# Factors of the second half of the rows: transposed x levelled on VectorE in place of transposes on TensorE

## The chip, the cores and the metric

The kernel runs on one core of a Trainium2 chip. The metric is the device time of one execution in microseconds, lower being better. The kernel before took 1429.79 us, the median of three runs (1428.46 to 1429.94). The kernel writes the output of the reference with a few extra steps on the host side that only permute and copy inputs.

## What is computed

x has 2048 rows of 576 numbers (float32). It is normalised row by row, and two branches are added to it:

```python
xn = _layernorm(x, axis=-1)                     # (x - mean) / sqrt(var + 1e-5)
A  = irfft2(rfft2(xn) * (w_r + 1j * w_i))       # over rows and columns
B  = (sigmoid(xn @ w_gate) * (xn @ w_up)) @ w_down
return x + A + B                                # w_gate, w_up: 576 x 4608; w_down: 4608 x 576
```

Nearly all the arithmetic is in branch B. Matrices are multiplied in float32 accuracy by splitting each operand into a rounded high part and a low part and adding three products (high·high, low·high, high·low).

## The kernel before

**Products.** The 4608 hidden columns are cut into 36 blocks of 128 (`NF`), the rows into two halves of 1024 (`PAIRS`); a half has two chunks of 512 rows (`CW`). A *unit* `u` is one hidden block for one half: units 0 to 35 are the first half, 36 to 71 the second. In a unit both w_gate and w_up times both chunks are formed with seven products in place of eight (a scheme of Strassen's kind): `PRODS` names the seven pairs of factors. The x side has the factors A11, A12, A21, A22 (chunk 1 or 2, column half 1 or 2) and the sums S1 = A21 + A22, S2 = S1 − A11, S3 = A11 − A21, S4 = A12 − S2. They lie transposed (columns on the partitions) as high and low parts in the fixed tile `X`; A21 and S3 share a slot, since A21 is read only by the first two blocks. The first two blocks of each half (units 0 and 1, 36 and 37) are done with plain products (`plain`, four products for each block and chunk); from the third on `unit` runs the seven (`made(0)` to `made(6)`). Each product is seven matmuls (line 635) into a PSUM bank: A and B have one buffer, E has two.

**Down-projection.** `down` multiplies the hidden activations of two blocks with w_down for 128 rows (line 742, 12 matmuls into a tile of the PSUM pair `pp`, which has two buffers); VectorE adds the result to the accumulator (line 746). The activations are made at the end of a unit: VectorE adds (line 719) and multiplies by the gate (720), ScalarE rounds the high part `hh` (725), VectorE subtracts for the low part `hl` (726). Plain products use lines 658, 662, 663 and 664 for this.

**Factors of the second half.** `second_pair` begins at unit 35 (`NF - 1`). It opens a new room of buffers (`room("x")`), loads eight tiles of 128 rows (line 347), and after three turns `blocks(1, c)` normalises them on ScalarE (`prep`, line 409), splits the remainder of 32 columns (lines 391 and 396) and calls `fill` for A11, A12, A21 and A22. `fill` transposes 256 rows of one factor on TensorE with the identity (lines 438 and 439, six transposes into a PSUM pair), and copies the result to `X`: ScalarE the high part (442, 443), VectorE the low part (444). From the second plain product of the second half on, `factors(1)` forms the sums on VectorE (lines 421 to 424) and fills S1 and S2; `late(1)` fills S3 and S4 when the plain products are done. That is 16 fills.

**Order of the work.** The order is written out by hand. Within a unit `beside(i)` runs after product `i`: it puts in down-projections (`spots`), then calls `turn`, which takes two steps of making the next weights (`make`), one of w_down (`wd`), then pending adds, then one step of each generator in `sides`. For the second half `make` is `get_w`, which loads split weights from scratch memory. On top of that, at build time each engine's instructions are put in a queue by a scheduler with estimated durations: it takes the earliest written instruction that it believes ready, so an instruction can run well before its written place. `keep_in_program_order` pins an instruction behind the one written just before it on its engine. All loads go through the one SyncE queue.

**Buffers.** During the first half the room holds `raw` (two buffers, raw weights of one block each) and `xa` (four buffers). From unit 4 to 32 the statistics of the second half's rows are made (`later_stats`), and at unit 32 mean and reciprocal deviation of all rows are written as rows to the scratch tensor `rowd`, which the Fourier branch reads as well. That branch's first stage opens its own room at unit 39 (`stage1`).

The x side of the products reads transposed x for the Fourier branch already from an input `xt`, laid out on the host.

Of the kernel before, what the change touches and what calls it, by code (L numbers as in the profile page):

```python
# [9 lines left out]
F32 = mybir.dt.float32  # L10
F32R = mybir.dt.float32r
I32 = mybir.dt.int32
AF = mybir.ActivationFunctionType
OP = mybir.AluOpType
PSUM = bass.MemoryType.PSUM

P = 128
S, D, F = 2048, 576, 4608
KD = D // 2 + 1
NQ = KD + 1  # L20
N1, N2 = 64, 32
NT = S // P
EPS = 1e-5
HD = D // 2
FR = HD + 1 - 2 * P
CW = 512
TPC = CW // P
PAIRS = S // (2 * CW)
TPP = 2 * TPC
KT = 2  # L30
REM = HD - KT * P
NF = F // P
# [5 lines left out]
KR = 3 * REM  # L38
# [88 lines left out]
def _layout(x, w_r, w_i, w_gate, w_up, w_down):  # L127

    ks = np.concatenate([np.arange(KT * P), np.tile(np.arange(KT * P, HD), 4)])
    w = np.stack([w_gate[COLS], w_up[COLS]]).reshape(2, 2, HD, NF, P)[:, :, ks]  # L130
    w = w[[1, 1, 0, 0], [0, 1, 1, 0]].reshape(4, KT + 1, P, NF, P).transpose(3, 2, 0, 1, 4)
    v = np.stack([w_r, w_i])[:, :, KOF].reshape(2, N1, N2 // 2, 2, KD).transpose(2, 1, 0, 3, 4)
    v = np.broadcast_to(v[:, None], (N2 // 2, 2, N1, 2, 2, KD))
    x = x.reshape(S, D)[ROWS][:, COLS]
    xt = x.reshape(NT, P, 2, HD)[..., ks].reshape(NT, P, 2, KT + 1, P).transpose(0, 4, 2, 3, 1)
    lay = {"x": x.reshape(NT, P, D), "xt": xt.reshape(NT, P, 2 * (KT + 1) * P), "ri": v.reshape(N2 // 2, P, 4 * KD),
           "w": w.reshape(NF, P, 4 * (KT + 1) * P), "wd": w_down[:, COLS].reshape(NF, P, D)}
    return {k: np.ascontiguousarray(a) for k, a in lay.items()}

# [5 lines left out]


@with_exitstack
def spectral_glu_kernel(ctx: ExitStack, tc: tile.TileContext, x, xt, ri, w_in, w_down, out):
    nc = tc.nc
    con = {k: nc.inline_tensor(v, name=f"c_{k}").ap() for k, v in _constants().items()}  # L150

    def f32(ap):
        return ap.bitcast(F32)
# [17 lines left out]
    X = fix.tile([P, NX, 5, CW], F32R, name="X")  # L171
    XA = {k: i for i, k in enumerate(("A11", "A12", "S3", "A22", "S1", "S2", "S4"))}
# [10 lines left out]
    rowd = tc.dram_tile([2, NT, P], F32, name="rowd")  # L183
# [27 lines left out]
    R = {}  # L211
    fp = ExitStack()

    def room(k):
        fp.close()
        R["pool"] = pool = fp.enter_context(tc.tile_pool(name=f"p{k}", bufs=1, side="right", reuse_waits="tile"))
        return pool
# [128 lines left out]
    def load_x(dst, t):  # L346
        nc.sync.dma_start(dst, x[t])
# [35 lines left out]
    XS, XR, RM = {}, {}, {}  # L383

    def new_xs(p, m):
        XS[m] = R["pool"].tile([P, 5, HD], F32, tag="xa", name=f"xa{p}_{m}", bufs=TPC)
# [28 lines left out]
    def prep(p, m, c):  # L415
        prep_hi(p, m, c)
        prep_lo(m, c)
# [12 lines left out]
    def fill(p, k, mm):  # L430

        i, j0 = XA[k], XP[k]
        cols = slice(2 * mm * P, (2 * mm + 2) * P)
        pt = pair(f"px{p}_{k}_{mm}")
        for j in range(2):
            m = 2 * mm + j
            for q in range(KT):
                nc.tensor.transpose(pt[:, 0, (2 * q + j) * P:(2 * q + j + 1) * P], XS[m][:, j0, q * P:(q + 1) * P], idf)
            nc.tensor.transpose(pt[:KR, 1, j * P:(j + 1) * P].bitcast(F32R), XR[m, j0], idr)
        v = pt[:, 0].rearrange("p (q s) -> p q s", q=KT)  # L440
        o = X[:, i, :, cols]
        nc.scalar.activation(o[:, :KT], v, AF.Copy)
        nc.scalar.activation(o[:KR, KT], pt[:KR, 1, :2 * P], AF.Copy)
        nc.vector.tensor_tensor(o[:, KT + 1:], v, f32(o[:, :KT]), op=OP.subtract)  # L444
# [476 lines left out]
    pend, adds, sides = [], [], []  # L921
# [18 lines left out]
    def blocks(p, c):  # L940
        for mm in range(2):
            for m in (2 * mm, 2 * mm + 1):
                prep(p, m, c)
            for k in (1, 2):
                fill(p, f"A{c + 1}{k}", mm)
            yield

    def second_chunk():

        yield from make_p(1)  # L950
        yield from blocks(0, 1)

    def second_pair():

        room("x")
        for m in range(TPC):
            new_xs(1, m)
        for c in range(2):
            for m in range(TPC):
                load_x(XS[m][:, 2 * c:2 * c + 2].rearrange("p a d -> p (a d)"), TPP + c * TPC + m)  # L960
        for _ in range(3):
            yield
        for c in range(2):
            yield from blocks(1, c)

    def factors(p):

        for mm in range(2):
            for m in (2 * mm, 2 * mm + 1):
                sums(p, m)  # L970
                yield
            for k in ("S1", "S2"):
                fill(p, k, mm)
                yield
            if mm == 0:
                sides.append(late(p))

    def late(p):

        while not done[p]:  # L980
            yield
        for mm in range(2):
            for k in ("S3", "S4"):
                fill(p, k, mm)
            yield

    done = [False, False]
# [30 lines left out]
    for p in range(PAIRS):  # L1018

        calls = [(0, 0), (1, 0), (0, 1), (1, 1)] if p == 0 else [(0, 0), (0, 1), (1, 0), (1, 1)]  # L1020
        for n, (f, c) in enumerate(calls):
            u = p * NF + f
            if p == 0 and n >= 2:
                wd = make_d(f)
            elif p and c == 0:
                wd = get_d(u)
            if p == 0 and n == 0:
                sides.append(second_chunk())
            if n == 2 - p:
                sides.append(factors(p))  # L1030
            if p == 0 and n == 3:
                make = make_w(G)
            elif p and n in (0, 2):
                make = get_w(u + 1)

            def beside(i):
                for _ in range((0, 0, 2, 2, 0)[i] if p and n < 2 else 0):
                    if pend:
                        adds.append(down(*pend.pop(0)))
                if i >= 0:  # L1040
                    turn(3 if p == 0 else 1)

            plain(u, c, beside)
            if p == 0 and n == 0:
                finish(*sides)
                sides.clear()
                load_raw(2)
            if p == 0 and n == 1:
                load_raw(3)
            finish(wd)  # L1050
            if n == 3:
                finish(make)
        done[p] = True
        late_input[0] = False
        pend = [(p, 0, m) for m in range(TPP)]

        for f in range(G, NF):
            u = p * NF + f

            spots = {i: 1 for i in (range(5) if f % G else range(4, 7))}  # L1060
            if u == NF + G:

                spots = {3: 2, 4: 2, 5: 2, 6: 2}
            elif u == LAST - 2:
                spots = {i: 1 for i in range(2, 7)}
                pend = [(p, f // G - 1, m) for m in range(TPP)]
                sides.append(gather())
            elif u == LAST - 1:
                spots = {i: 1 for i in range(3)}
            if u + 1 < LAST:  # L1070
                make = make_w(u + 1) if u + 1 < NF else get_w(u + 1)
            if u < NF and f % G == 0:
                wd = make_dt(f // G)
            if p == 0 and f and f % 4 == 0:
                sides.append(later_stats(TPP + f // 4 - 1))
            if u == NF - 1:
                sides.append(second_pair())

            def beside(i):
                nonlocal step, rounds  # L1080
                if (u, i) == (NF + G + 1, 5):
                    rounds = seven()
                for _ in range(spots.get(i, 0)):
                    if pend:
                        adds.append(down(*pend.pop(0)))
                for a in extra.get((u, i), ()):
                    a()
                if i < 0:
                    return
                if u > NF + G:  # L1090
                    next(rounds, None)
                turn(2 if u + 1 < NF else 1)
                if u > NF + G:
                    active.extend(b() for b in begin.pop(step, []))
                    step += 1
                    aside()

            unit(u, beside)
            finish(make)
            if f % G == G - 1:  # L1100
                finish(wd)
            if u == NF + G:
                lower("b")
            if u + 2 < NF:
                load_raw(u + 2)
            if p == 0 and f % G == G - 1:
                pend = [(p, f // G, m) for m in range(TPP)]
# [30 lines left out]
```

## Time and profile before

| what | value |
|---|---|
| median of three runs | 1429.79 us (1428.46 to 1429.94) |
| the profiled execution's own time | 1428.53 us |
| its span, first to last instruction | 1426.7 us |
| mean granted TensorE clock | 0.998 |
| unit 34 starts / unit 35 starts / first product of unit 38 | 615.65 / 631.55 / 696.51 us |
| transposes of the second half's factors, first and last start | 644.33 / 701.87 us |

The profile comes from one execution on the chip. Times are microseconds from the first instruction; PE is TensorE, PEld its weight loads, DVE VectorE, ACT ScalarE, SP SyncE's queue. Matmuls overlap, so two neighbours in the timeline start closer together than one lasts: rates are read from start to start. In a wait row, the engine and line on the left stood idle until the one on the right was done.

### The profile page before, as it was taken

Reading aid. Unit: us, or ns where it says so; the run is one execution under the profiler, and the core shown is the slowest. Engines: PE = TensorE matmul, PEld = TensorE weight load, DVE = VectorE, ACT = ScalarE, POOL = GpSimd, SP = SyncE. Lnnn points to the kernel's source line nnn. Section 1 sums busy time; section 2 is a strip of 40 time slices with the busy share of each in tenths; the row PEclk is TensorE's granted clock in tenths of the full one; section 3 lists DMA queues with packets and bytes.
Section 4 is the critical chain, followed back from the end, with each engine's and each line's share of the span. In section 5 each row is a group of like instructions: output and inputs, shape, how many; then the busy total and the mean of one; then the engine's idle time right before and its main releaser. Section 6 shows DMA issues by size and latency. Waiting matters only on the chain. (4 is left out here: it accounts for less than half of the span.)

```text
span 1426.7 us, 20983 instructions
## 1 busy us (share of the span) xinstructions
PE 1412.8 (99%) x7979; PEld 1243.9 (87%) x7979; DVE 1097.7 (77%) x1734; ACT 651.2 (46%) x1075; POOL 3.3 (0%) x5
## 2 busy tenths in 40 slices
PE   8999999999999999999999999999999999999998
PEld 5888888888888888888888888888888889998997
DVE  7988888888888888766366888877888877766784
ACT  6644444444444444454335544534555534444431
POOL 0000000000000000000000000000000000000000
PEclk9999999999999999999999999999999999999999
DMA  6488677777777775564667777778888787776642
GB/s 249 192 329 309 257 270 264 271 262 270 265 262 265 256 265 223 224 262 149 233 215 231 232 217 236 217 250 261 274 267 274 239 284 232 234 222 199 200 126 83
DMA packets 130676, 341.41 MB, mean 239 GB/s; under 512 B 12144, under 2 KB 51600, under 8 KB 125712
## 3 DMA queue, kind: packets, MB, share of 16 engines
q1 hardware_dynamic: 129648, 338.76, 70.4%
q8 instruction: 63, 1.03, 0.3%
q10 hardware_dynamic: 928, 1.31, 0.3%
q14 instruction: 37, 0.30, 0.1%
HBM read 203.89 MB, written 136.13 MB: 238 GB/s over the span
## 5 line engine op out<-in xcount | busy, mean ns | idle before, releaser
L635 PE MATMUL pB<-X,w 128*128 128x512 f32 x1484 | 380.6, 393 | 0.0
L635 PEld LDWEIGHTS pB<-X,w 128*128 128x128 f32 x1484 | 267.6, 188 | 49.4 <-ACT v L699 1.3
L635 PE MATMUL pE<-X,w 128*128 128x512 f32 x1064 | 272.3, 392 | 0.0
L635 PE MATMUL pA<-X,w 128*128 128x512 f32 x1008 | 260.1, 394 | 1.8 <-DVE X L444 1.2
L635 PEld LDWEIGHTS pE<-X,w 128*128 128x128 f32 x1064 | 193.1, 188 | 34.2
L635 PEld LDWEIGHTS pA<-X,w 128*128 128x128 f32 x1008 | 184.0, 189 | 35.4 <-DVE X L444 1.9
L742 PE MATMUL po<-wd,hh 128*128 128x288 f32 x1216 | 210.9, 295 | 0.0
L833 PEld LDWEIGHTS ps<-wf,hs 128*128 128x128 f32 x1260 | 189.0, 188 | 17.8 <-ACT qs L841 0.9
L833 PE MATMUL ps<-wf,hs 128*128 128x288 f32 x1260 | 202.1, 295 | 0.4 <-ACT qs L841 0.4
L742 PEld LDWEIGHTS po<-wd,hh 128*128 128x128 f32 x1216 | 184.4, 188 | 11.3
L746 DVE TENSOR_TENSOR acc<-acc,po 128x576 f32<-128x576 f32 x168 | 125.9, 750 | 76.7 <-PE po L742 75.5
L239 ACT ACTIVATE w<-raw 128x768 fp32r<-128x768 f32 (+1 forms) x106 | 100.9, 953 | 92.7 <-PE pE L635 36.5
L742 PE MATMUL po<-wd,hl 128*128 128x288 f32 x608 | 128.9, 293 | 0.0
L843 DVE TENSOR_TENSOR qs<-qs,ps 128x576 f32<-128x576 f32 x112 | 84.1, 751 | 28.3 <-PE ps L833 27.5
L742 PEld LDWEIGHTS po<-wd,hl 128*128 128x128 f32 x608 | 98.8, 189 | 0.0
L700 DVE TENSOR_TENSOR y<-v,pE 128x512 f32<-128x512 f32 x68 | 46.8, 688 | 52.3 <-ACT v L699 51.3
L843 DVE TENSOR_TENSOR acc<-acc,ps 128x576 f32<-128x576 f32 x90 | 67.6, 751 | 23.2 <-PE ps L833 22.6
L241 DVE TENSOR_TENSOR w<-raw,w 128x512 fp32r<-128x512 f32 (+1 forms) x106 | 81.9, 773 | 3.2 <-ACT w L239 2.9
L720 DVE TENSOR_TENSOR y<-y,g 128x1024 f32<-128x1024 f32 x67 | 81.9, 1223 | 3.2
L769 ACT ACTIVATE hs<-y 128x512 fp32r<-128x512 f32 x105 | 64.8, 629 | 37.8 <-DVE y L720 14.6
L703 ACT ACTIVATE g<-pB 128x512 f32<-128x512 f32 x68 | 40.6, 598 | 90.4 <-PE pB L635 90.2
L699 ACT ACTIVATE v<-pB 128x512 f32<-128x512 f32 x68 | 40.6, 598 | 71.2 <-PE pB L635 70.7
(162 smaller groups left out, 1636.2 us busy)
## 6 DMA issues: line engine op xcount, KB each, us to landing
w<-wsp SPq DMA_DIRECT2D x246, 320.0 KB, 3.5
wsp<-w SPq DMA_DIRECT2D x34, 2240.0 KB, 7.7
raw<-in_w SPq DMA_DIRECT2D x34, 768.0 KB, 9.7
wdsp<-wd SPq DMA_DIRECT2D x36, 576.0 KB, 4.7
wf<-tsp SPq DMA_DIRECT2D x60, 288.0 KB, 3.8
wf<-wdsp SPq DMA_DIRECT2D x45, 288.0 KB, 3.9
std<-in_wd SPq DMA_DIRECT2D x36, 288.0 KB, 5.5
ri<-in_ri SPq DMA_DIRECT2D x16, 578.0 KB, 5.2
```

The source lines that it names most:

```text
L239: placed(nc.scalar.activation(o[:, :, :3, :], src, AF.Copy))
L241: placed(nc.vector.tensor_tensor(o[:, :, 3:, :], src[:, :, :KT, :], f32(o[:, :, :KT, :]), op=OP.subtract))
L635: nc.tensor.matmul(bank, w[:, sw, :], X[:, x, sx, :], start=start and j == 0, stop=stop and j == len(STEPS) - 1, skip_group_check=skip)
L699: nc.scalar.activation(v[:, 1], bank["B"], AF.Copy)
L700: nc.vector.tensor_tensor(y[:, 1], v[:, 1], bank["E"], op=OP.add)
L703: nc.scalar.activation(g[:, 1], bank["B"], AF.Sigmoid)
L720: nc.vector.tensor_tensor(y, y, g, op=OP.mult)
L742: nc.tensor.matmul(pd[:, b, :HD], h[i], w[k][b], start=g == 0 and n == 0, stop=g == G - 1 and n == 2)
L746: nc.vector.tensor_tensor(a, a, pd[:, :, :HD], op=OP.add)
L769: nc.scalar.activation(hs[:, 0], src, AF.Copy)
L833: nc.tensor.matmul(pd[:, i, :HD], h[:, a, m], w[:, b], start=q == 0, stop=q == 2)
L843: nc.vector.tensor_tensor(o, o, pd[:, :, :HD], op=OP.add)
```

## The change

A second layout of transposed x for the second half of the rows, `xg`, is an input: for each chunk and column half the columns on the partitions and the chunk's 512 rows along the free dimension, two blocks of 128 columns and one with the remainder of 32 columns repeated four times. The raw numbers are loaded and normalised where they lie: mean and reciprocal deviation of the 512 rows are read from `rowd` onto all partitions (`load_rows`), and VectorE subtracts and multiplies (`level`). `put` writes high and low parts into `X`; `second_factors` forms the sums on the transposed data. No transposes remain for the second half, and `room("x")` is not opened: chunk 0 and the rows of both chunks lie in the `xa` buffers (`spare`), chunk 1 in the two `raw` buffers (`load_whole`). The first chunk is loaded at the start of unit 34 and levelled in its turns 2 to 5; the rows of chunk 1 and its second column half are loaded at the start of unit 35, where chunk 1 is levelled and A11, A12, A21, A22 are put, each after the product that last reads its slot. S1, S2 and S4 follow beside the plain products, S3 after them.

```diff
--- before.py
+++ after.py
@@ -133,7 +133,8 @@
     v = np.broadcast_to(v[:, None], (N2 // 2, 2, N1, 2, 2, KD))
     x = x.reshape(S, D)[ROWS][:, COLS]
     xt = x.reshape(NT, P, 2, HD)[..., ks].reshape(NT, P, 2, KT + 1, P).transpose(0, 4, 2, 3, 1)
-    lay = {"x": x.reshape(NT, P, D), "xt": xt.reshape(NT, P, 2 * (KT + 1) * P), "ri": v.reshape(N2 // 2, P, 4 * KD),
+    xg = xt[TPP:].reshape(2, TPC, P, 2, KT + 1, P).transpose(0, 3, 2, 4, 1, 5).reshape(2, 2, P, (KT + 1) * CW)
+    lay = {"x": x.reshape(NT, P, D), "xt": xt.reshape(NT, P, 2 * (KT + 1) * P), "xg": xg, "ri": v.reshape(N2 // 2, P, 4 * KD),
            "w": w.reshape(NF, P, 4 * (KT + 1) * P), "wd": w_down[:, COLS].reshape(NF, P, D)}
     return {k: np.ascontiguousarray(a) for k, a in lay.items()}
 
@@ -145,7 +146,7 @@
 
 
 @with_exitstack
-def spectral_glu_kernel(ctx: ExitStack, tc: tile.TileContext, x, xt, ri, w_in, w_down, out):
+def spectral_glu_kernel(ctx: ExitStack, tc: tile.TileContext, x, xt, xg, ri, w_in, w_down, out):
     nc = tc.nc
     con = {k: nc.inline_tensor(v, name=f"c_{k}").ap() for k, v in _constants().items()}
 
@@ -950,18 +951,103 @@
         yield from make_p(1)
         yield from blocks(0, 1)
 
+    XG, XGR, MR, WHOLE = {}, {}, {}, {}
+
+    def spare(name):
+        t = R["pool"].tile([P, 5, HD], F32, tag="xa", name=name, bufs=TPC)
+        return t.rearrange("p a d -> p (a d)")[:, :2 * CW].rearrange("p (a s) -> p a s", a=2)
+
+    def load_rows(c):
+        MR[c] = spare(f"mr{c}")
+        for i in range(2):
+            v = rowd[i, TPP + c * TPC:TPP + (c + 1) * TPC].rearrange("t p -> (t p)")
+            nc.sync.dma_start(MR[c][:, i], v.partition_broadcast(P))
+
+    def level(c, *aps):
+        m, r = MR[c][:, 0], MR[c][:, 1]
+        for a in aps:
+            like = [v[:a.shape[0]] if len(a.shape) == 2 else v.unsqueeze(1).to_broadcast(a.shape) for v in (m, r)]
+            tc.keep_in_program_order(nc.vector.tensor_tensor(a, a, like[0], op=OP.subtract))
+            nc.vector.tensor_tensor(a, a, like[1], op=OP.mult)
+
     def second_pair():
 
-        room("x")
-        for m in range(TPC):
-            new_xs(1, m)
-        for c in range(2):
-            for m in range(TPC):
-                load_x(XS[m][:, 2 * c:2 * c + 2].rearrange("p a d -> p (a d)"), TPP + c * TPC + m)
+        load_rows(0)
+        rem = None
+        for h in range(2):
+            XG[0, h] = spare(f"xg0_{h}")
+            nc.sync.dma_start(XG[0, h].rearrange("p k s -> p (k s)"), xg[0, h, :, :KT * CW])
+            if rem is None:
+                rem = spare("xgr")
+            XGR[0, h] = rem[:KR, h]
+            nc.sync.dma_start(XGR[0, h], xg[0, h, :KR, KT * CW:])
+        load_whole(0)
         for _ in range(3):
             yield
-        for c in range(2):
-            yield from blocks(1, c)
+        for h in range(2):
+            level(0, XG[0, h])
+            yield
+            level(0, XGR[0, h])
+            yield
+
+    def load_whole(h):
+        t = R["pool"].tile([P, 4, 3, P], F32, tag="raw", name=f"xg1_{h}", bufs=2)
+        t = t.rearrange("p b k f -> p (b k f)")
+        nc.sync.dma_start(t, xg[1, h])
+        WHOLE[h] = t = t.rearrange("p (k s) -> p k s", s=CW)
+        XG[1, h], XGR[1, h] = t[:, :KT], t[:KR, KT]
+
+    def second_chunk_of_pair():
+
+        load_rows(1)
+        load_whole(1)
+        yield
+        put("A11", XG[0, 0], XGR[0, 0])
+        level(1, WHOLE[0])
+        yield
+        yield
+        level(1, WHOLE[1])
+        yield
+        put("A12", XG[0, 1], XGR[0, 1])
+        yield
+        put("A21", XG[1, 0], XGR[1, 0])
+        yield
+        put("A22", XG[1, 1], XGR[1, 1])
+
+    def put(k, a, b):
+
+        o, r = X[:, XA[k]], slice(2 * REM, 3 * REM)
+        nc.scalar.activation(o[:, :KT], a, AF.Copy)
+        nc.scalar.activation(o[:KR, KT], b, AF.Copy)
+        nc.vector.tensor_tensor(o[:, KT + 1:], a, f32(o[:, :KT]), op=OP.subtract)
+        nc.vector.tensor_tensor(o[r, KT], b[r], f32(o[r, KT]), op=OP.subtract)
+
+    def second_factors():
+
+        A11, A12, A21, A22 = ((XG[c, h], XGR[c, h]) for c in range(2) for h in range(2))
+
+        def both(o, a, b, op):
+            for i in range(2):
+                nc.vector.tensor_tensor(o[i], a[i], b[i], op=op)
+
+        both(A22, A21, A22, OP.add)
+        yield
+        put("S1", *A22)
+        yield
+        both(A21, A11, A21, OP.subtract)
+        yield
+        both(A11, A22, A11, OP.subtract)
+        yield
+        put("S2", *A11)
+        yield
+        both(A12, A12, A11, OP.subtract)
+        yield
+        put("S4", *A12)
+        yield
+        while not done[1]:
+            yield
+        put("S3", *A21)
+        yield
 
     def factors(p):
 
@@ -1027,7 +1113,7 @@
             if p == 0 and n == 0:
                 sides.append(second_chunk())
             if n == 2 - p:
-                sides.append(factors(p))
+                sides.append(second_factors() if p else factors(p))
             if p == 0 and n == 3:
                 make = make_w(G)
             elif p and n in (0, 2):
@@ -1073,8 +1159,9 @@
                 wd = make_dt(f // G)
             if p == 0 and f and f % 4 == 0:
                 sides.append(later_stats(TPP + f // 4 - 1))
-            if u == NF - 1:
-                sides.append(second_pair())
+            if u in (NF - 2, NF - 1):
+                sides.append(second_pair() if u == NF - 2 else second_chunk_of_pair())
+                next(sides[-1])
 
             def beside(i):
                 nonlocal step, rounds
```

## The prediction

> **What bounds the kernel now.** I read the page first: the span and the engine lines.
>
> ```profile
> span 1426.7 us, 20983 instructions
> PE 1412.8 (99%) x7979; PEld 1243.9 (87%) x7979; DVE 1097.7 (77%) x1734; ACT 651.2 (46%) x1075; POOL 3.3 (0%) x5
> ```
>
> TensorE is busy 99% of the span. That share says little by itself, so I next cut the time around the change into stretches: unit 34 (the last product but one of the first half) starts at 615.65, unit 35 at 631.55; the plain products of the second half follow, and unit 38 is the first seven-product unit after them. Columns: stretch, its length, busy time and instructions of PE, PEld, DVE, ACT, POOL, the granted clock, DMA share, GB/s.
>
> ```profile
> 0.00:100.00 100.00, 92.28 (x479) 76.11 (x480) 83.84 (x179) 60.33 (x110) 3.29 (x5) 0.98 0.68 250
> 615.65:620.41 4.76, 4.76 (x23) 3.94 (x21) 4.41 (x5) 2.72 (x3) 0.00 (x0) 1.00 0.30 122
> 620.41:631.55 11.14, 11.14 (x65) 10.00 (x64) 7.64 (x13) 3.87 (x6) 0.00 (x0) 1.00 0.53 210
> 631.55:644.33 12.78, 12.78 (x79) 11.60 (x77) 6.90 (x12) 9.42 (x14) 0.00 (x0) 1.00 0.82 285
> 644.33:650.60 6.27, 6.27 (x48) 5.65 (x47) 4.04 (x8) 3.83 (x11) 0.00 (x0) 1.00 0.21 73
> 650.60:663.69 13.09, 13.09 (x81) 11.30 (x81) 12.78 (x31) 8.03 (x22) 0.00 (x0) 1.00 0.46 158
> 631.55:703.67 72.12, 72.12 (x437) 63.75 (x435) 39.95 (x76) 33.49 (x72) 0.00 (x0) 1.00 0.58 195
> ```
>
> From 615.65 to 703.67 TensorE has no gap and the clock is 1.00. So each TensorE instruction taken out there is time taken off, unless a wait comes in. Third, the same stretch for the tiles px_A and px_S (what the transposes write), the transposes themselves, and the TensorE timeline.
>
> ```profile
> 631.55:703.67 72.12, 5.88 (x48) 4.87 (x48) 5.37 (x8) 6.71 (x16) 1.00 0.58 195
> 631.55:703.67 72.12, 5.45 (x48) 5.05 (x48) 5.21 (x8) 6.71 (x16) 1.00 0.58 195
> L438 PE MATMUL px_A<-idf,xa x64: 270/273/328, 10.4 to 655.9; 128*128 128x128 f32 x64
> ```
>
> ```profile
> 615.65 1.75 PE L635 MATMUL pA<-X,w 128*128 128x512 f32 x7
> 617.24 1.75 PE L635 MATMUL pE<-X,w 128*128 128x512 f32 x7
> ...
> 631.55 1.77 PE L635 MATMUL pA<-X,w 128*128 128x512 f32 x7
> ...
> 641.13 1.77 PE L635 MATMUL pA<-X,w 128*128 128x512 f32 x7
> ...
> 644.33 0.38 PE L438 MATMUL px_A<-idf,xa 128*128 128x128 f32 x2
> ...
> 644.89 0.68 PE L635 MATMUL pB<-X,w 128*128 128x512 f32 x2
> ...
> 645.97 1.36 PE L635 MATMUL pB<-X,w 128*128 128x512 f32 x5
> ...
> 703.67 1.75 PE L635 MATMUL pA<-X,w 128*128 128x512 f32 x7
> ```
>
> 48 and 48: all 96 transposes of the second half lie here, 16 fills of six. They are in the bounding queue.
>
> **What goes: the transposes.** One product (seven matmuls) takes 617.24 − 615.65 = 1.59 us. From 631.55 to 641.13 stand three products, each with one down-projection: 9.58 / 3 = 3.193 us a pair. From 631.55 to 703.67 there are 26 products (7 of unit 35, 16 plain, 3 of unit 38) and 13 down-projections (5 and 8). Without transposes: 13 × 3.193 + 13 × 1.59 = 41.5 + 20.7 = 62.2 us. The stretch took 72.12, so the transposes cost 9.9 us, 103 ns each. The direct row agrees from below: six take 644.89 − 644.33 = 0.56 us, 16 × 0.56 = 9.0; the rest is the slower first matmul after each block. I take 9.9.
>
> The length of one transpose in its row is 273 ns, since neighbours overlap. The Trainium skill ("TensorE: Matmul & The Clock Gate", section "Part 4: PE-mode transpose") gives about 275 ns for a 128×128 transpose in a kernel; by that 96 would be worth about 26 us. The row has the same length, but the starts in the timeline are 93 to 103 ns apart, so the trace does not bear that sum out as throughput. The same section says that transposes do not count as busy for the clock; no stretch above shows a clock below 1.00 with them in it.
>
> **What comes: work on VectorE.** Prices come from the groups kept apart by shape (last two numbers before the bar's idle time: total us, mean ns).
>
> ```profile
> L746 DVE TENSOR_TENSOR acc<-acc,po 128x576 f32<-128x576 f32 x168 | 125.9, 750 | 76.7 <-PE po L742 75.5 <-DMA am<-c_am 0.8
> L720 DVE TENSOR_TENSOR y<-y,g 128x1024 f32<-128x1024 f32 x67 | 81.9, 1223 | 3.2
> L241 DVE TENSOR_TENSOR w<-raw,w 128x512 fp32r<-128x512 f32 x72 | 49.5, 687 | 0.8 <-ACT w L239 0.5
> L241 DVE TENSOR_TENSOR w<-raw,w 128x768 fp32r<-128x768 f32 x34 | 32.4, 954 | 2.4 <-ACT w L239 2.4
> L322 DVE TENSOR_TENSOR wtl<-wt,wth 128x1152 fp32r<-128x1152 f32 x15 | 20.3, 1353 | 0.5 <-ACT wth L320 0.5
> L243 DVE TENSOR_TENSOR w<-raw,w 32x384 fp32r<-32x384 f32 x34 | 18.6, 549 | 0.7
> L444 DVE TENSOR_TENSOR X<-px_A,X 128x512 fp32r<-128x512 f32 x16 | 10.7, 688 | 3.5 <-ACT X L443 3.4
> L396 DVE TENSOR_TENSOR rma<-xa,rma 128x64 fp32r<-128x64 f32 x24 | 4.9, 220 | 3.5 <-ACT rma L391 3.5
> L725 ACT ACTIVATE hh<-y 128x1024 fp32r<-128x1024 f32 x34 | 36.0, 1059 | 10.3 <-DVE y L720 10.3
> ```
>
> - Levelling chunk 0: for each half of the columns a subtraction and a multiplication of 1024 and of 512 elements: 2 × (2 × 1.223 + 2 × 0.687) = 7.6 us, at turns 2 to 5 of unit 34.
> - Levelling chunk 1: four instructions of 1536. From 768 and 1152 (0.399 us for 384 more) that is 1.75 each, 7.0 us, in unit 35.
> - Each of seven puts: 1.223 plus a 32x512. The latter I put at the 687 of 128x512 (32x384 takes 549): 1.9 us. Four in unit 35: 7.6 us.
> - Four sums and differences (each 1024 and 512): 4 × 1.91 = 7.6 us, from the second plain product on, with three more puts, 5.7 us.
>
> In all 35.5 us on VectorE, most of it off the path if the queue holds. What falls away there is 16 remainders of 512 from PSUM (the 5.37 and 5.21 us above) and the small pieces of lines 396 and 421 to 424. ScalarE gets seven copies of 1.06 and seven of some 0.6 us, 11.6 us, and loses 32 copies (6.71 + 6.71) and the normalisations: less than before, so no cost.
>
> **The place that can lose it.** From turn 2 of unit 34 (620.41) to the end of unit 35 without its transposes (631.55 + 5 × 3.193 + 2 × 1.59 = 650.7) there are 30.2 us. VectorE's present work in the three stretches is 7.64 + 6.90 + 4.04 = 18.6, of which 4.3 goes away (two L444 of 0.69 and 0.2 of a third, four L421 of 0.46 and four L396 of 0.22). Remaining 14.3, plus 22.2 new: 36.5 us of work in 30.2. VectorE leaves unit 35 about 6.3 us late. Then the first plain product (four pairs, 12.8 us) holds 7.5 us of its own (four adds of 0.75, lines 719, 720, 726, 662, 664), which gives 5.3 back; the second holds 12.0 in 12.8, and the third 7.1 in 6.4. Who waits for that queue?
>
> ```profile
> 639.93 0.46 DVE L421 TENSOR_TENSOR xa<-xa 128x288 f32<-128x288 f32 x1 [0.63 <-ACT xa L409]
> 656.16 1.22 DVE L720 TENSOR_TENSOR y<-y,g 128x1024 f32<-128x1024 f32 x1
> 658.64 1.23 DVE L726 TENSOR_TENSOR hl<-y,hh 128x1024 fp32r<-128x1024 f32 x1
> 660.51 0.69 PE L742 MATMUL po<-wd,hh 128*128 128x288 f32 x4
> ```
>
> ```profile
> PE pA L635 <- DVE X L444: 1.2, 2, 0.8
> PE b L891 <- DMA idr<-c_id: 3.7, 1, 3.7
> ```
>
> The down-projections of the first plain product need hl of unit 35: line 726 ends at 659.87, the first starts at 660.51 and its hl matmuls half a microsecond later, so the slack is about 1.0 us. Taken in written order TensorE would wait 6.3 − 1.0 = 5.3 us. But the queues are not in written order: line 421 ran at 639.93, though it is written behind the second plain product's first quarter; and at 644.89 and 645.97 one product is split, two matmuls ahead of a block of transposes that wait for a PSUM pair and five behind. Products that need neither hl nor an add can so be drawn ahead: the last of the first plain product and the four of the second, 5 × 1.59 = 8.0 us, more than 6.3. The stretch 650.60 to 663.69 shows it possible: VectorE at 12.78 of 13.09 us, TensorE without a gap. Bounds of this wait: 0 and 5.3 (a wait below zero is excluded, TensorE has none to lose). I take 1.2, the only wait of TensorE for VectorE-made factors among the rows, in the first half.
>
> **Loads and queue.** SP now issues two broadcast rows, two halves and two remainders of chunk 0 and the first whole half of chunk 1 in front of unit 34, and the rest at unit 35: 3968 KB against 8 × 288 = 2304, so 1664 KB (1.7 MB) more. From 615.65 to 650.60 the rows moved 0.58 + 2.34 + 3.64 + 0.46 = 7.0 MB; 8.7 MB in 34.95 us is 250 GB/s, under the 285 reached from 631.55 to 644.33. Cost 0, hidden by products. The rows of chunk 1 reuse the buffer of chunk 0's, so their load waits until levelling of chunk 0 is done (some 635.7 by the tally), and behind it on SP stand unit 36's weights, wanted at 650.7.
>
> ```profile
> w<-wsp SPq DMA_DIRECT2D x246, 320.0 KB, 3.5
> raw<-in_w SPq DMA_DIRECT2D x34, 768.0 KB, 9.7
> am<-c_am SPq DMA_DIRECT2D x16, 256.0 KB, 2.7
> mb<-rowd SPq DMA_DIRECT2D x16, 64.0 KB, 5.1
> ```
>
> A weight block lands 3.5 us after issue, so they are in time if SP is held no longer than about 10 us. The room that is no longer opened costs nothing: the region is then released by the last put, where before the last transposes released it.
>
> **Sum.** Against the profiled execution, 1428.53 us (span 1426.7): 1428.53 − 9.9 + 1.2 = 1419.8. The median of the three runs, 1429.79, lies 1.26 above it: 1421.1 us, 0.6% faster.
>
> **Rivals.**
> 1. VectorE becomes the bound and its order is kept as written: TensorE waits 5.3 us at the first down-projections. 1429.79 − 9.9 + 5.3 = 1425.2. For it: 36.5 us of work in 30.2. Against: the reordering above.
> 2. Slower: the broadcast rows of chunk 1 land late, and the levelling waits in VectorE's queue with adds and hl behind it. They are wanted some 5 us after issue (behind the put of A11, lines 720 and 726). The bounds for 2 × 256 KB: 2.7 us (am, 256 KB) and 41 us (mb by its bytes, 64 KB in 5.1). Between them I take 5.1, what a load of this kind took here, and not 41, since raw's 768 KB land in 9.7. Landing in L, TensorE waits 5.3 + L − 5; the gain is used up at L = 9.6 and the kernel is measurably slower from L = 12.5. At L = 20 it is 1429.79 − 9.9 + 20.3 = 1440. The one wait of that kind above, 3.7 us at the start, stands in a stretch of clock 0.98, at most 2 us lost. The same page of the Trainium skill (section "What's actually happening") says that an idle window of about 3.4 us halves the clock; in the stretches above there is no such window to show it.
> 3. Transposes are worth their full length: 96 × 0.273 = 26.2 us, 1403.6. Only the 273 speaks for it; the 72.12 us stretch has no room for it.
>
> That the transposes were hidden and their removal does nothing is excluded by the gapless TensorE row.
>
> **How the numbers follow.** Forecast 0.58 (1418.5 to 1423.5), first rival 0.20 (1423.5 to 1428.5), second 0.18, third 0.04. The range that leaves out the second and third is 1417.5 to 1428.5. About 0.2% (2.9 us) is what a measurement of this kernel can tell. Faster: 0.58 + 0.04 + 0.13 of the first rival = 0.75; the same: 0.07 of it and 0.02 of the second, 0.09; slower 0.16.
>
> **What would show it.** No px tile after 600 us; unit 35's start to the fourth product of unit 38 in 62 to 64 us; VectorE above 90% from 620 to 665; products drawn ahead of down-projections there; waits of TensorE on hl (line 726) or acc (746) below 2 us in all. The prediction is wrong if TensorE shows gaps of over 5 us between 635 and 690, behind levelling that waits for the broadcast rows, or if weights of unit 36 land after 651.

## The result and the profile after

The changed kernel takes 1421.41 us (median of 4 runs, 1419.66 to 1421.72) against 1429.33 us of the kernel before: a ratio of 0.9943, 95% interval 0.9925 to 0.996. The forecast was 1421.1.

The page of the changed kernel begins as follows. There are 96 matmuls fewer, VectorE is busy 15 us longer, ScalarE 11 us shorter.

```profile
span 1419.8 us, 20725 instructions
PE 1405.9 (99%) x7883; PEld 1235.9 (87%) x7883; DVE 1112.5 (78%) x1722; ACT 640.6 (45%) x1035; POOL 3.3 (0%) x5
```

The stretches around the change (columns as in the prediction): about unit 34; the part where VectorE was to be fullest; and from the start of unit 35 to the start of `made(3)` in unit 38, the stretch that took 72.12 us before.

```profile
617.00:632.94 15.94, 15.94 (x86) 13.81 (x85) 15.59 (x21) 6.59 (x9) 0.00 (x0) 1.00 0.39 162
620.00:665.00 45.00, 44.54 (x243) 38.30 (x242) 44.19 (x51) 17.17 (x25) 0.00 (x0) 1.00 0.51 165
632.94:696.43 63.49, 63.03 (x340) 54.53 (x339) 51.77 (x60) 22.73 (x32) 0.00 (x0) 1.00 0.67 212
```

VectorE is at 98% (44.19 of 45.00 us) from unit 34 into the plain products of unit 36, and TensorE still runs almost without a gap. The stretch is 8.63 us shorter. Without transposes its products and down-projections were worked out at 62.2 us, so 9.9 us went and 1.3 us came; both figures hang on these 62.2. TensorE's timeline shows where:

```profile
632.94 1.77 PE L636 MATMUL pA<-X,w 128*128 128x512 f32 x7
...
648.93 1.86 PE L636 MATMUL pB<-X,w 128*128 128x512 f32 x7
650.62 1.75 PE L636 MATMUL pA<-X,w 128*128 128x512 f32 x7
652.83 1.89 PE L636 MATMUL pE<-X,w 128*128 128x512 f32 x7 [0.46 <-DVE y L701]
654.55 1.76 PE L636 MATMUL pA<-X,w 128*128 128x512 f32 x7
656.15 1.75 PE L636 MATMUL pE<-X,w 128*128 128x512 f32 x7
657.74 0.69 PE L743 MATMUL po<-wd,hh 128*128 128x288 f32 x4
...
659.32 1.77 PE L636 MATMUL pE<-X,w 128*128 128x512 f32 x7
661.01 0.98 PE L636 MATMUL pA<-X,w 128*128 128x512 f32 x3
661.96 1.31 PE L743 MATMUL po<-wd,hh 128*128 128x288 f32 x8
...
696.43 1.75 PE L636 MATMUL pA<-X,w 128*128 128x512 f32 x7
```

The last product of unit 35 (pE at 652.83) waits for line 701, which must read bank E before this product adds to it. Ahead of it stands already a pA of the first plain block, at 650.62: it is written later. From 648.93 to 654.55 the three products take 5.62 us, 0.85 more than 3 × 1.59. The down-projections are taken apart too: at 657.74 run the halves that need unit 34's activations only, then products, and from 661.96 the halves that need unit 35's. On VectorE, in the same profile:

```profile
652.08 0.69 DVE L701 TENSOR_TENSOR y<-v,pE 128x512 f32<-128x512 f32 x1
...
657.29 0.69 DVE L720 TENSOR_TENSOR y<-v,pE 128x512 f32<-128x512 f32 x1
657.89 1.22 DVE L1031 TENSOR_TENSOR xg<-xg,xg 128x1024 f32<-128x1024 f32 x1
659.03 1.22 DVE L721 TENSOR_TENSOR y<-y,g 128x1024 f32<-128x1024 f32 x1
...
661.94 1.23 DVE L727 TENSOR_TENSOR hl<-y,hh 128x1024 fp32r<-128x1024 f32 x1
```

Line 727 ends at 663.17; the matmuls that read hl follow at 663.34. A sum of the second factors (line 1031) is drawn ahead of line 721. It takes 1.22 us, but line 721 starts 1.14 us behind it: in a full VectorE queue too, start to start is shorter than the length.

Between two profiled executions there is also a difference that has nothing to do with the change: the granted clock of the first 25 us (the runs below show 0.86 or 0.93 with the changed kernel, and 0.86 or 1.00 with the kernel before). Before, then after:

```profile
0.00:25.00 25.00, 18.46 (x75) 13.40 (x76) 16.58 (x59) 12.22 (x25) 3.29 (x5) 0.93 0.72 254
0.00:25.00 25.00, 19.04 (x70) 13.58 (x71) 15.95 (x57) 11.50 (x25) 3.29 (x5) 0.86 0.69 245
```

Unit 34 starts at 616.82 after and at 615.65 before, 1.17 us later. That is most of why the spans differ by only 6.9 us while the stretch lost 8.63; unit 34 itself, where chunk 0 is levelled, takes another 0.2 us longer (16.12 against 15.90). Below, stretches are compared with stretches.

### The profile page after: what moved, and what is told of

Same layout as the page of the kernel before. It is cut to its first block, busy times and chain, and to the rows that moved or that the text cites. A ratio compares the mean times of both kernels' runs of the same rounds, so it can differ in the third digit from the quotient of the medians.

```text
span 1419.8 us, 20725 instructions
## 1 busy us (share of the span) xinstructions
PE 1405.9 (99%) x7883; PEld 1235.9 (87%) x7883; DVE 1112.5 (78%) x1722; ACT 640.6 (45%) x1035; POOL 3.3 (0%) x5
```

## Experiments

The theory after the trace: the gain is the transposes' place in TensorE's queue; VectorE's surplus is covered because TensorE's queue draws later work ahead, and this cover is a reserve that is nearly spent. The rivals: the gain comes from something else; VectorE does not matter; written order would have done as well. The table gives each run's stretch from the start of unit 35 to `made(3)` of unit 38, from its timeline, and its time. A ratio is taken to runs of the kernel before from the same series, whose medians lie between 1428.39 and 1429.54 us.

| run | stretch us | time us (median) | ratio to before (95%) |
|---|---|---|---|
| before | 631.55 to 703.67: 72.12 | 1429.33 | |
| changed | 632.94 to 696.43: 63.49 | 1421.41 | 0.9943 (0.9925 to 0.996) |
| transposes twice, on before | 633.07 to 714.16: 81.09 | 1437.94 | 1.006 (1.0043 to 1.0077) |
| written order, on changed | 633.22 to 700.09: 66.87 | 1424.16 | 0.9968 (0.9956 to 0.998) |
| written order, on before | 631.36 to 704.54: 73.18 | 1430.41 | 1.0009 (0.9999 to 1.0018) |
| 7 us more on VectorE | 632.84 to 700.66: 67.82 | 1425.07 | 0.9972 (0.9962 to 0.9982) |
| 14 us more on VectorE | 631.58 to 706.27: 74.69 | 1431.61 | 1.0023 (1.0014 to 1.0032) |
| rows loaded three times | 631.91 to 698.51: 66.60 | 1424.70 | 0.9971 (0.996 to 0.9982) |
| chunk 1 levelled on GpSimd | 631.32 to 703.88: 72.56 | 1429.05 | 1.0001 (0.9992 to 1.001) |
| chunk 0 spread over two units | 631.52 to 695.13: 63.61 | 1421.14 | 0.9945 (0.9933 to 0.9958) |
| late puts | 633.06 to 695.96: 62.90 | 1420.55 | 0.9937 (0.9923 to 0.995) |
| spread and late puts | 631.55 to 694.32: 62.77 | 1419.56 | 0.9937 (0.9924 to 0.9949) |

### The transposes twice

```diff
 # kernel before, fill()
-        for j in range(2):
+        for j in [0, 1] * (1 + p):
```

> The kernel before, with each of the 96 transposes of the second half issued twice into the same PSUM tile; nothing else changes. If a transpose costs TensorE its place in the queue (the prediction's 9.9 us for 96), the time rises by 9 to 10 us over the kernel before, to about 1439. If it costs its full length of 273 ns, it rises by 26 us. If the transposes lay beside other work and the gain of the change came from elsewhere (the loads, the room), it rises by less than 3 us.

The time rose from 1428.59 to 1437.94, by 9.35 us; the stretch by 8.97. First and last rows of the stretch:

```profile
633.07 1.77 PE L635 MATMUL pA<-X,w 128*128 128x512 f32 x7
...
714.16 1.75 PE L635 MATMUL pA<-X,w 128*128 128x512 f32 x7
```

8.97 / 96 = 93 ns for a transpose, the start-to-start time of the timeline before. The 0.9 us between this and the 9.9 that left the stretch fit the slower first matmul after each block, which doubling a block does not repeat. So the transposes were on the path at their pitch, neither hidden nor at 273 ns. The Trainium skill's 275 ns ("TensorE: Matmul & The Clock Gate", section "Part 4: PE-mode transpose") is a length, as the row's 273 is, and no price in a full queue.

### Written order on TensorE

```diff
 # both kernels; pinned from unit 34 to unit 38
+    def pin(ins):
+        if pinned[0]:
+            tc.keep_in_program_order(ins)
 # prod() and down()
-    nc.tensor.matmul(...)
+    pin(nc.tensor.matmul(...))
```

> The changed kernel, with all product and down-projection matmuls of units 34 to 38 pinned to their written order on TensorE. If the surplus of VectorE is covered because TensorE's queue draws products ahead of down-projections, this cover goes, and TensorE waits 4 to 9 us more: 1425 to 1430, the gain half or wholly gone. If VectorE's surplus does no harm in any order, the time stays within 1 us of the changed kernel's 1421.4.

> The kernel before with the same pins, as the control. The theory of the cover: VectorE has no surplus here, so the pins cost little, 0 to 2 us over the kernel before. If the pins cost by themselves (written order is bad whatever VectorE does), it loses as much as the changed kernel does with them.

The changed kernel loses 3.4 us in the stretch with the pins, the kernel before 1.1. The time of the first, 1424.16, lies just below the range expected; half or all of the gain was to go, and some 60% of it is left (5.25 of 8.63 us in the stretch). TensorE's waits in the pinned changed kernel's stretch (total, times, longest):

```profile
PE po L749 <- ACT hh L732: 1.7, 1, 1.7
PE pE L642 <- DVE y L707: 1.7, 1, 1.7
PE po L749 <- DVE hl L733: 0.5, 1, 0.5
```

They are the two places of the unpinned timeline: bank E behind the levelling (line 707 there is 701 of the changed kernel), and hh and hl of unit 35. The stretch is 4.7 us over the 62.2 of its matmuls, against 1.3 with the free queue. So the queue's freedom is worth 3.4 us here, and written order alone does not lose the gain. VectorE's lateness is not the whole of a pin's cost: the kernel before pays 1.1 us too, 0.6 of it in transposes that wait for a PSUM pair.

### More work for VectorE

```diff
 # changed kernel, level(); n = 2 or 4
             nc.vector.tensor_tensor(a, a, like[1], op=OP.mult)
+            for _ in range(n if c == 1 else 0):
+                nc.vector.tensor_tensor(a, a, a, op=OP.max)
```

> The changed kernel with two further instructions of 128x1536 behind each levelling of chunk 1 (the maximum of the tile with itself, which leaves the numbers as they are): 4 x 1.75 = 7.0 us more of VectorE work in unit 35. By the prediction's tally (6.3 us late, 8.0 us of cover) TensorE waits 5.3 us more: 1426.7. By the trace of the changed kernel, where the first product of the second plain block started at 661.01 just behind the release of its bank, the cover is already used up: the full 7 us more, 1428.4. If VectorE is not on the path at all: 1421.4.

> The changed kernel with four further instructions behind each levelling of chunk 1, 14.0 us more of VectorE work in unit 35 (7.0 us more cost 3.7). If the cover is a fixed reserve of some 3 us that is now used up, the second 7 us cost their full length: 3.7 + 7 = 10.7, about 1432. If TensorE goes on finding half as much work to draw ahead, 7.4: about 1429.

7 us more lengthened the stretch by 4.33, 14 us more by 11.20. The lengths overstate the work added: back to back these instructions start 1.67 us apart, so it is 6.7 and 13.3 us. How late VectorE became shows at line 701, with 7 and with 14 us more:

```profile
658.28 0.69 DVE L701 TENSOR_TENSOR y<-v,pE 128x512 f32<-128x512 f32 x1
663.69 0.69 DVE L701 TENSOR_TENSOR y<-v,pE 128x512 f32<-128x512 f32 x1
```

From the start of unit 35 that is 25.44 and 32.11 us, against 652.08 − 632.94 = 19.14 in the changed kernel: 6.3 and 13.0 us later. So 2.0 and 1.8 us of the lateness did not reach TensorE's time. That the two nearly agree looks like a fixed reserve, as the expectation for 14 us put it, but the losses of 4.33 and 11.20 are not waits alone. The stretch with 7 and with 14 us more, with the granted clock third from the end:

```profile
632.84:700.66 67.82, 64.66 (x340) 55.79 (x339) 58.44 (x64) 22.75 (x32) 0.00 (x0) 0.97 0.62 197
631.58:706.27 74.69, 65.80 (x340) 56.92 (x339) 65.04 (x68) 22.89 (x32) 0.00 (x0) 0.93 0.55 179
```

The same 340 matmuls keep TensorE busy for 64.66 and 65.80 us, against 63.03 in the changed kernel, where the clock was 1.00. In steps of 0.1 us the granted clock stands at 0.50 from 664.3 to 667.8 in the first run and from 655.7 to 666.0 in the second, 3.4 and 10.2 us. Busy time times the share of the clock withheld, added up over the steps, gives 1.7 and 3.2 us. Without them TensorE lost 2.6 and 8.0 us, so it found 3.7 and 5.0 us more work to draw ahead: more where VectorE is later, and half clock takes part of it back. With 7 us more both readings beforehand were off: the time lies under the 1426.7 of the tally and the 1428.4 of the trace. With 14 us more it came out as for a fixed reserve, 1431.61 for some 1432, though not for that reason alone. TensorE with 7 us more, and SyncE's queue:

```profile
655.92 1.43 PE L636 MATMUL pA<-X,w 128*128 128x512 f32 x5 [0.92 <-DVE X L1024]
...
663.95 0.87 PE L636 MATMUL pB<-X,w 128*128 128x512 f32 x2 [2.24 <-DMA w<-wsp]
```

```profile
660.95 1.75 SPq L287 DMA_DIRECT2D w<-wsp x4
```

TensorE's order here is not that of the changed kernel: it is set at build time, with the added work in the scheduler's estimates. The queue reaches further than the prediction allowed: at 663.95 it starts the third plain block (pB, unit 37). There it waits 2.24 us for that unit's weights, whose load was issued at 660.95 only, since they reuse the buffer of unit 35's weights and the last product of unit 35 was late. A late VectorE so becomes a late load, and 0.4 us after this wait the clock falls to half.

### The broadcast rows late

```diff
 # changed kernel, load_rows()
-            nc.sync.dma_start(MR[c][:, i], v.partition_broadcast(P))
+            for _ in range(3 if c else 1):
+                nc.sync.dma_start(MR[c][:, i], v.partition_broadcast(P))
```

> The changed kernel with the two broadcast rows of chunk 1 loaded three times, one load behind the other, so that they land some 10 us later (6.6 us is the median from issue to landing). The prediction's second rival: TensorE waits for each microsecond over what the cover holds; by its formula with a landing at 17 us the time is about 1437, by the milder loss seen with 7 us more of VectorE work (3.7 us of 7) about 1427. If the landing of these rows does not matter, 1421.4.

VectorE begins levelling chunk 1 at 646.53, 14.62 us after unit 35 starts, in place of 641.44 − 632.94 = 8.50:

```profile
646.53 3.43 DVE L971 TENSOR_TENSOR xg<-xg,mr 128x1536 f32<-128x1536 f32 x2 [4.08 <-DMA mr<-rowd]
```

It is 6.1 us later, not the 10 expected, and the stretch 3.1 us longer; the time, 1424.70, lies under both the 1437 and the 1427 of the expectation. Part of the idle time is made good, since two adds that stood between the four levellings run before them; line 701 is 4.8 us later (655.84 − 631.91 = 23.93 against 19.14), and 1.7 us of that did not reach TensorE's time. Here too half clock is part of the loss: it lasts from 656.5 to 660.0 and costs 1.7 us, after a wait of 2.33 us for the put of A12. The stretch, a part of it, and the product that starts that part:

```profile
631.91:698.51 66.60, 64.26 (x340) 55.80 (x339) 52.23 (x60) 22.89 (x32) 0.00 (x0) 0.97 0.72 218
656.58:658.20 1.62, 1.62 (x4) 1.33 (x5) 1.62 (x2) 0.00 (x0) 0.00 (x0) 0.50 0.00 0
656.58 3.35 PE L636 MATMUL pE<-X,w 128*128 128x512 f32 x7
```

The next matmul starts at 659.74, 3.16 us behind the start of this product in place of 1.59. The prediction's second rival has the right mechanism; it counted each microsecond from a landing of 5 us on as lost.

### Chunk 1 levelled on GpSimd

```diff
 # changed kernel, level()
+            eng = nc.gpsimd if c else nc.vector
-            tc.keep_in_program_order(nc.vector.tensor_tensor(a, a, like[0], op=OP.subtract))
-            nc.vector.tensor_tensor(a, a, like[1], op=OP.mult)
+            tc.keep_in_program_order(eng.tensor_tensor(a, a, like[0], op=OP.subtract))
+            eng.tensor_tensor(a, a, like[1], op=OP.mult)
```

> The changed kernel with chunk 1 levelled on GpSimd, which is idle here: 7.0 us of VectorE work leave unit 35. If VectorE's lateness is all that is lost, the stretch falls to 62.3 us and the kernel to about 1420.2, as long as GpSimd is done with the first half by 654 and the second by 656, where the puts of A21 and A22 stood. No row shows GpSimd's price; four instructions started at about 641 may take 3.5 us each. If they take longer, the puts of A21 and A22 come late and the second plain block waits: 1422 to 1430.

The whole gain is gone, and not because GpSimd is late: it is done at 654.73. GpSimd's four instructions, then VectorE in the same time:

```profile
638.70 4.20 POOL L971 TENSOR_TENSOR xg<-xg,mr 128x1536 f32<-128x1536 f32 x1 [634.88 <-DVE X L1024]
642.97 3.52 POOL L972 TENSOR_TENSOR xg<-xg,mr 128x1536 f32<-128x1536 f32 x1
646.43 4.47 POOL L971 TENSOR_TENSOR xg<-xg,mr 128x1536 f32<-128x1536 f32 x1
650.98 3.75 POOL L972 TENSOR_TENSOR xg<-xg,mr 128x1536 f32<-128x1536 f32 x1
```

```profile
643.58 3.99 DVE L1023 TENSOR_TENSOR X<-xg,X 128x1024 fp32r<-128x1024 f32 x1 [1.73 <-ACT X L1021]
647.49 0.74 DVE L747 TENSOR_TENSOR acc<-acc,po 128x576 f32<-128x576 f32 x1
648.27 3.18 DVE L1024 TENSOR_TENSOR X<-xgr,X 32x512 fp32r<-32x512 f32 x1
651.48 4.33 DVE L1023 TENSOR_TENSOR X<-xg,X 128x1024 fp32r<-128x1024 f32 x1
```

The three puts take 3.99, 3.18 and 4.33 us where they take 1.22, 0.68 and 1.22 otherwise: each ends 0.55 to 1.08 us after the GpSimd instruction that ran when it started (646.49, 650.90, 654.73). The add of line 747, which reads one side from PSUM, takes its usual 0.74 inside a GpSimd instruction. Relieving VectorE of 7.0 us cost it 8.4 us of standing still (11.5 against 3.1), all of it ahead of line 701.

Line 701 starts at 655.73, 5.3 us later than in the changed kernel, and the stretch is 9.1 us longer. Nothing of that is covered: the order on TensorE has no later product ahead of the one that needs line 701, where the changed kernel has a pA and the run with 7 us more has over two products. TensorE waits 6.46 us there, and its clock is at half from 652.1 to 662.3, which costs it 2.9 us of work:

```profile
656.46 3.35 PE L636 MATMUL pE<-X,w 128*128 128x512 f32 x7 [6.46 <-DVE y L701]
631.32:703.88 72.56, 65.43 (x340) 56.76 (x339) 53.96 (x56) 22.75 (x32) 15.87 (x4) 0.93 0.57 186
```

That the scheduler, at build time, took VectorE to be relieved and so drew nothing ahead is likely from this order, and not shown by a run.

### Chunk 0 spread, and late puts

```diff
 # spread: loads at unit 33, half h of chunk 0 levelled in turns 2 and 3 of unit 33 + h
-        load_whole(0)
-        for _ in range(3):
-            yield
         for h in range(2):
+            for _ in range(3 + 2 * h):
+                yield
 # spread, further down: where the units are gone through
-            if u in (NF - 2, NF - 1):
-                sides.append(second_pair() if u == NF - 2 else second_chunk_of_pair())
+            if u in (NF - 3, NF - 1):
+                sides.append(second_pair() if u == NF - 3 else second_chunk_of_pair())
                 next(sides[-1])
+            if u == NF - 2:
+                load_whole(0)
 # late puts
         put("A12", XG[0, 1], XGR[0, 1])
         yield
+        yield
+        yield
+        yield
         put("A21", XG[1, 0], XGR[1, 0])
```

> The changed kernel with chunk 0 loaded at the start of unit 33 and its two column halves levelled in units 33 and 34 (turns 2 and 3 of each) in place of both in unit 34; 3.8 us of VectorE work leave unit 34. If the 1.3 us that the stretch from unit 35 to unit 38 lasts over its 62.2 us of products are VectorE's lateness, most of them go: the stretch falls to 62.3 to 62.8 us and the time by 0.5 to 1.2 us, to about 1420.5. If they come from something else (the weight loads, the mixed order of products and down-projections), the stretch stays at 63.5.

> The changed kernel with the puts of A21 and A22 written into the first plain product (after its first and second quarter) in place of behind the fifth and sixth product of unit 35; the second plain block needs them only some 10 us later. If the 1.3 us lost are the burst of puts ahead of lines 720, 721 and 727, the wait on hh and hl goes; the earlier wait on line 701 (0.5 us at 652.8), which stands behind the levelling, stays: the stretch falls from 63.5 to 62.7 to 63.1 us. If the order of the puts does not matter, 63.5.

> Chunk 0 spread over units 33 and 34 as in the run with the spread, and the puts of A21 and A22 late as well. The theory of two places (levelling ahead of line 701, puts ahead of lines 720, 721 and 727): with both relieved the stretch comes to 62.2 to 62.6 us and the time to about 1420.2, 1 us under the changed kernel. If the loss is not VectorE's queue but the mixed order of products and down-projections, it stays at 63.5 us.

The spread alone changed nothing (63.61): the expectation was wrong. Line 701 came 1.9 us earlier in its unit (648.76 − 631.52 = 17.24), but this time no pA stands ahead of the product that needs it, which starts 0.4 us late all the same, at 649.50. TensorE then waited on hh, in the spread kernel

```profile
658.63 1.32 PE L743 MATMUL po<-wd,hh 128*128 128x288 f32 x8 [0.67 <-ACT hh L726]
```

since the puts of A21 and A22 still stood ahead of lines 720 and 721. Late puts alone gave 62.90, as expected; both together 62.77, with one wait left, of 0.29 us on line 727:

```profile
657.47 0.53 PE L743 MATMUL po<-wd,hl 128*128 128x288 f32 x2 [0.29 <-DVE hl L727]
```

That is slightly over the 62.2 to 62.6 expected. So of the 1.3 us lost, 0.7 are VectorE's order around the end of unit 35; of the other 0.6, half is this last wait, and the rest stays open. Both kernels have a ratio of 0.9937 to before; against the changed kernel's 0.9943 that lies inside the intervals, and only the stretches tell them apart.

## Why the prediction was right

- **The transposes, 9.9 us.** Shown by two runs: they left the stretch (72.12 to 63.49 with 1.3 us of new loss), and twice as many cost 8.97 in the stretch and 9.35 in the time. With the waits relieved as far as they were, the stretch came to 62.77, 0.5 over the tally of 62.2 that the term rests on. The prediction's remark that no stretch shows a clock below 1.00 with transposes in it holds for these 96, and also for twice as many; its first row, 0.98 from 0 to 100 us, has transposes of the first half in it.
- **The wait, 1.2 us.** Measured 1.3 over the tally, so the size was right, by luck: the row it was taken from, a wait of the first half, was not the reason. Some 0.85 us was lost around line 701 through bank E, which the prediction did not name, and about 0.5 at hh and hl. The spread and late puts together recover 0.7 of it.
- **VectorE 6.3 us late.** Its queue was full, 44.19 of 45.00 us from 620 to 665. Line 720, which follows the last put of unit 35, starts at 657.29, 5.2 us after the end of unit 35 by the tally (632.94 + 5 × 3.193 + 2 × 1.59 = 652.1). The tally added lengths, and instructions in a full queue start closer together than that, so 6.3 was too much. The cover was put at 8.0 us, which left 1.7 in reserve; in three runs 2.0, 1.8 and 1.7 us of lateness did not reach TensorE's time. That this agrees is partly luck: the queue found 3.4 to 5.0 us more to draw ahead than in the changed kernel, from the third plain block among others, and the clock at half, which the prediction named only for late rows, took 1.7 to 3.2 of it back.
- **The first rival (written order, 5.3 us of waits, 1425.2).** With the order pinned: 4.7 us over the tally, 1424.16, though not all at the first down-projections: 2.2 us are waits for hh and hl, 1.7 the wait on line 707, and up to 1.1 may be the price of the pins themselves. So it was the free order that decided between the forecast and this rival.
- **The second rival (late rows).** The load was issued at 635.67 (worked out: 635.7, but with unit 35 starting 1.39 us earlier than it did here), both rows had landed by 641.44, 5.8 us later (taken: 5.1), and VectorE waited 0.3 us for them. Each microsecond over was priced as lost in full, and the run with late rows shows 1.7 of 4.8 covered. The loss of clock that the rival bounded at 2 us did come in that run, 1.7 us, after a wait of 2.33 us, shorter than the window it quotes.
- **Loads, the room, ScalarE: nothing.** No wait of TensorE in the changed kernel's stretch names a load. Its weight loads name ScalarE with 0.7 us (hh 0.4 and the gate 0.3), at places where ScalarE runs behind VectorE.

The forecast was hit within 0.3 us, but the starting clock alone moves a run by over 1 us, so the agreement of the terms is better evidence than that of the sum.

## What to carry to other kernels

In a full TensorE queue a small matmul costs its start-to-start time, here 93 ns against a length of 273: read it from the timeline, and check it by issuing it twice. Moving its work to another engine pays as long as that engine's lateness stays within the work that the bounding queue can draw ahead. Adding work in two doses shows how near the edge a kernel is; here some 2 us of lateness were free, and the rest counted in full. Before such a sum is read as waits alone, the granted clock of the stretch should be read: a third of the loss or more was half clock in two of the three runs. The order in the queue is made at build time, so a helper engine that turns out slower than the scheduler believed may find no cover at all, as with GpSimd. An average load of 78% said nothing of this; the burst of 98% at one place, and what stands behind it in the queue, decided.

## What was not expected of the hardware

A running GpSimd instruction stops VectorE. A VectorE instruction with two inputs in SBUF that started while GpSimd ran a subtraction or multiplication took 3.2 to 4.3 us in place of 0.7 to 1.2, and ended about its own length after GpSimd's; one with an input in PSUM took its usual 0.74. The Trainium skill ("SBUF — State Buffer", section "Who interferes with whom") says that a VectorE instruction with two SBUF inputs contends with a GpSimd one that reads SBUF, that the shared ports are an exclusive lock for which the order of issue decides who blocks, and that a VectorE instruction with at most one SBUF input, outside the 2-port modes, does not contend. The rows agree: in all three cases the later one, VectorE's, stood still. Whether GpSimd is held in its turn they do not settle. An idle GpSimd was no spare capacity here.

TensorE's clock fell to half during a long wait or soon after it. In the four runs in which TensorE waited 2.24, 2.33, 5.58 and 6.46 us at one place, the granted clock was 0.50 for 3.4, 3.4, 10.2 and 10.2 us. In the other eight profiled runs, both kernels among them, TensorE waited 1.7 us at most, and the clock stayed at 1.00 through the stretch. The length of a wait does not decide alone: with 14 us more, a later wait of 2.31 us (for weights, until 671.22) was not followed by a fall. What decides beside it, no run here shows.
